# mLSTM cell and tanh-shrink MLP: four more attention units in the split form, another division of the value products, and a re-ranked plan

## The chip, the cores and the metric

One core of a Trainium2 chip. The metric is the device time of one execution in microseconds (us). The kernel before was run three times: 518.15, 518.27 and 518.37 us, median 518.27.

## The reference

Two blocks follow each other. The first is an mLSTM cell over batch 4, 8 heads, 768 steps and head size 40; the second takes the cell's output as 3072 rows of 320 features through two weight matrices with x - tanh(x) between them. All data is float32.

```python
for t in range(S):
    m_new = np.maximum(f_gate[:, :, t] + m, i_gate[:, :, t])
    f_stab = np.exp(f_gate[:, :, t] + m - m_new)
    i_stab = np.exp(i_gate[:, :, t] - m_new)
    C = f_stab * C + i_stab * outer(vt, kt)
    n = f_stab * n + i_stab * kt
    y[:, :, t] = sigmoid(o_gate[:, :, t]) * (C @ qt) / max(abs(n @ qt), 1.0)
x = y.transpose(0, 2, 1, 3).reshape(B * S, H * D)      # (3072, 320)
h = x @ w_in                                           # (3072, 2048)
out = (h - np.tanh(h)) @ w_out                         # (3072, 320)
```

The kernel computes the cell in chunks of 128 steps: scores of queries against keys, masked to earlier steps, times scaled values, plus queries times the state that the earlier chunks left. For small h it takes h - tanh(h) from a polynomial; a branch at the end repeats everything in another way where the bounds do not hold, and is not entered with these inputs.

## The kernel before

**Units.** The cell's work is cut into 24 units: unit n is chunk n // 4 of batch n % 4, all 8 heads, 128 steps. Its steps on TensorE are the scores (`ps`, from `kz` and `qz`), the second products, the update of the state (`pc`, from `k` and the scaled values `vs`), and the turning of the result `ys` into features first, `xT`. DVE or POOL mask the scores into `P`; DVE divides and applies the output gate.

**Two forms.** Units 0 to 11 take the plain form: `inter` and `intra` sum state and values into `ph` (tokens in the rows), `gate` divides, and three transposes on TensorE (`turn`, tile `px`) with a copy (`keep_x`) give `xT`. Units 12 to 23 take the split form: the state is kept with the heads' halves in rows 0 to 39 and 64 to 103; `block_turned` forms values times `P` the other way round (tile `pT`); `turn_back` brings that to tokens in the rows through a round trip by memory (`h_rows`, `z_in`), `gate_turned` divides, and `turn_by_store` makes `xT` by another round trip (`y_rows`). Every one of these transfers is issued on SP's queue. `in_halves` brings the states of the four batches from the plain layout to the split one; it is called four times where the loop begins.

**The MLP.** 12 groups of 256 rows; per group 8 pairs of 128 hidden columns. An item is the up product of one or two pairs (tile `ph_up`): for two pairs 8 products over all 128 rows of the array and 4 over the remaining 64 features, which run in row halves, two at a time. With `quarters`, an item before `block_turned` runs its last part in quarters of the array. The shrink is two squarings on ACT (`z`, `q`) and two products on DVE (`gt`), which also free the banks of `ph_up` for the next item. The down product is `po` (plain) or `pS` (seven products in place of eight, with sums of the weights `wT` and of `gt`, tiles `s`).

**The order.** A helper fixes the order of instructions on each engine to that in which they are written. The first part of it comes from `Plan`: steps with a cost, a rank, their forerunners and the banks that they take are laid out by a small model (`plan.run`, line 1490), and are written out in that order. It covers units 0 to 11, the conversion of the weights (which come as 64-bit numbers) and items 0 to 16. Behind it stands a loop from item 17 (`START`) on, with two items a unit: in the first the new unit is scored after the item's up products, in the second `block_turned` follows the up products. Between the two, line 1510 asks for the loads of the loop's first unit, and lines 1511 and 1512 bring the states into halves:

```python
    load_unit(PLANNED, ("kz", "qz", "v", "k", "o"))
    for b in range(B):
        in_halves(b)
```

Within the loop, the loads of the next unit are asked for at the start of a unit (`cell_slot`).

**Queues.** SP issues the loads of the units and all transfers of the split form, in the written order; an issue whose data is not ready holds what stands behind it. POOL issues the loads of the weights and selects masks for the units in `BY_POOL`. ACT issues most of the output.

**Names in the code.** `weights` and `plan_weights` (conversion, `product` is its last step), `block_turned`, `turn_back`, `turn_by_store`, `in_halves`, `up`, `plan_unit`, `plan_item`, and the constants from line 1182 on.

Of the kernel before, what the change touches and what calls it, by code (L numbers as in the profile page):

```python
# [49 lines left out]
FP = mybir.dt.float32  # L50
# [29 lines left out]
def kernel(  # L80
# [76 lines left out]
    class Plan:  # L157
# [5 lines left out]
        COLD, TURN, WAIT = (6.2, 1.8), 0.12, 0.2188  # L163
# [346 lines left out]
    def weights(dst, srcs, queue):  # L510
# [41 lines left out]
        def product():  # L552
            V.tensor_tensor(out=dst, in0=w["r"], in1=w["e"].bitcast(FP), op=OP.mult)
# [5 lines left out]
    def blocks_of(p):  # L559
# [9 lines left out]
        for i in range(2):  # L569
            whole.append((slice(i * HALF, (i + 1) * HALF), slices(4, 1), moe_w_in[half[i]:half[i] + HALF, slices(2 * p + i, 1)]))  # L570
        return (weights(w_in[:, p, :], whole, G),
                weights(w_out[:, 2 * p:2 * p + 2, :].rearrange("p two n -> p (two n)"),
                        [(every, slice(0, 2 * DM), moe_w_out[slices(2 * p, 2), :].rearrange("(two p) n -> p two n", two=2))], G))
# [40 lines left out]
    def scaled(n, i, name, bufs, by_heads=False):  # L614

        t = un[n]
        flat = att.tile([L, H * D1 + HALF - D1], FP, name=name, tag=name, bufs=bufs)
        to = flat[:, 0:H * D1].rearrange("p (h d) -> p h d", d=D1)
        t["wide"] = flat
        scale = ei[:, i, t["c"], t["hs"]]  # L620
        t["column"] = lambda: A.copy(out=to[:, :, D], in_=scale)
        if by_heads:
            for h in range(H):
                A.mul(out=to[:, h, 0:D], in_=t["v"][:, h], mul=scale[:, h:h + 1])
        else:
            V.tensor_tensor(out=to[:, :, 0:D], in0=t["v"], in1=scale.unsqueeze(2).to_broadcast([L, H, D]), op=OP.mult)
        return to
# [107 lines left out]
    def turn_by_store(n):  # L735
# [6 lines left out]
        V.transpose(flat[:, 0:NK * 128], y[:, 0:NK * 128])  # L742
        V.transpose(flat[:, NK * 128:], y[:, FROM[NK]:])
        rows = dram.tile([(NK + 1) * 128, L], FP, name="y_rows", tag=f"y_rows{n % 4}")
        for a in range(L // BLOCK):
            part = slice(a * BLOCK, (a + 1) * BLOCK)
            SP.dma_start(out=rows[:, part].rearrange("(b i) j -> i b j", i=BLOCK), in_=yt[part])
        for i in range(2):
            half = slice(i * HALF, (i + 1) * HALF)
            SP.dma_start(out=xT[g % NX][half, :, tt * L:(tt + 1) * L], in_=rows.rearrange("(c p) t -> p c t", p=128)[half])  # L750

    def in_halves(b):


        old, new = (state[b][i].rearrange("p h d -> p (h d)") for i in (1, 0))
        for h in (0, 1, 2, 4, 5, 6, 7):
            i, j = divmod(h, HH)
            r = h % TRIO
            n = 2 if h == 0 else 1
            to, at = (x[:, first * D1:(first + TRIO * (n - 1) + 1) * D1].rearrange("p (h d) -> p h d", d=D1)[:, ::TRIO]  # L760
                      for x, first in ((new, j), (old, h)))
            SP.dma_start(out=to[i * HALF:i * HALF + D], in_=at[r * D:(r + 1) * D])

    def block_turned(n):
# [4 lines left out]
        G.memset(t["wide"][:, H * D1:], 0.0)  # L769
        old = state[t["b"]][(t["c"] + 1) % 2].rearrange("p h d -> p (h d)")  # L770

        t["turned"] = [ps_a.tile([128, 2 * 2, L], FP, name="pT", tag=f"a{i}") for i in range(2)]
        for g in range(2):
            for c in range(2):
                for i in range(2):
                    rows, j = slice(i * HALF, i * HALF + D), 2 * g + c
                    T.matmul(t["turned"][i][c * HALF:(c + 1) * HALF, i * 2 + g, :], old[rows, j * D1:j * D1 + HALF], t["qz"][rows, j, :],
                             start=(g == 0), stop=False, skip_group_check=True)
        for i in range(2):
            for g in range(2):  # L780
                for c in range(2):
                    for r in range(2):
                        rows, j = slice(r * HALF, (r + 1) * HALF), 2 * g + c
                        at = (i * HH + j) * D1
                        T.matmul(t["turned"][r][c * HALF:(c + 1) * HALF, i * 2 + g, :], t["wide"][rows, at:at + HALF], t["P"][rows, i, j, :],
                                 start=False, stop=True, skip_group_check=True)
        update_halves(n)

    def update_halves(n):
        t = un[n]  # L790
# [16 lines left out]
    def turn_back(n):  # L807
# [3 lines left out]
        both = att.tile([128, 2, HH * L // BLOCK, BLOCK], FP, name="zt", tag="P", bufs=4)  # L811
        zt, added = both[:, 0], both[:, 1].rearrange("p b i -> p (b i)")
        flat = zt.rearrange("p b i -> p (b i)")
        A.copy(out=added, in_=t["turned"][1].rearrange("p g t -> p (g t)"))
        V.tensor_tensor(out=added, in0=t["turned"][0].rearrange("p g t -> p (g t)"), in1=added, op=OP.add)
        V.transpose(flat, added)
        rows = dram.tile([2, 2, HH, L, BLOCK], FP, name="h_rows", tag=f"h_rows{n % 4}")
        for a in range(128 // BLOCK):
            half, low = divmod(a, 2)
            SP.dma_start(out=rows[low, half].rearrange("g (b k) i -> k (g b) i", k=BLOCK), in_=zt[a * BLOCK:(a + 1) * BLOCK])  # L820
        t["z"] = att.tile([L, 2, H, BLOCK], FP, name="z_in", tag="P", bufs=4)
        for i in range(4):
            part = slice(i * BLOCK, (i + 1) * BLOCK)
            SP.dma_start(out=t["z"][part].rearrange("t a h i -> t (a h) i"),
                         in_=rows.rearrange("a c g t i -> t (a c g) i")[part])
# [27 lines left out]
    def cell_slot(s, o):  # L853
# [16 lines left out]
        steps.append((0.0, lambda: turn_by_store(o)))  # L870
# [152 lines left out]
    def up(some, shrink, quarters=False):  # L1023
# [16 lines left out]
        def quarter(i, x, c):  # L1040
            g, p = some[x]
            rows, cols, first = slice(i * HALF, (i + 1) * HALF), slice(c * HALF, (c + 1) * HALF), 2 * NK * 128 + c * HALF
            T.matmul(ph[i][cols, x, :], w_in[rows, p, first:first + HALF], xT[g % NX][rows, ((0, 2, 1), (0, 1, 2))[i][NK], :],
                     start=False, stop=True, skip_group_check=True)

        full = [(0.43, lambda i=i, x=x, j=j: product(i, x, j)) for i in range(2) for x in range(n) for j in range(NK)]
        if quarters:
            rest = [lambda i=i, x=x, c=c: quarter(i, x, c) for x in range(n) for c in range(2) for i in range(2)]
        else:
            rest = [lambda i=i, x=x: product(i, x, NK) for x in range(n) for i in range(2)]  # L1050
# [132 lines left out]
    SCALED, SHARED = (7, 11), (3, 5, 7, 8, 9, 10, 11)  # L1183
    RANKS = (-1.0, -1.0, -8.2006, -8.4463, 6.0242, 2.3893, 9.5327, 2.6415, 25.6922, 13.6176, 29.7021, 7.061)
    WEIGHTS = (0.08, -0.3563, 5.1266, 7.6972, 9.6586, 11.6503, 11.1391, 25.4848)
    START = item(FIRST * NP)
    HOLD = 43.9795
    FETCH = {(0, 1): 6.75, (2, 1): 12.25, (3, 0): 19.87, (3, 1): 31.49}
    APART = ()
    BY_POOL = (2, 5, 6, 7, 8, 9)  # L1190
# [56 lines left out]
    LATE = {"o": -2.69, "k": -3.541, "q2": -4.0692, "v": -1.3038}  # L1247

    def plan_unit(n, rank):
# [17 lines left out]
        else:  # L1267
# [3 lines left out]
            if c:  # L1271
# [14 lines left out]
        u["scores"] = plan.add("T", 1.0, first_part, [u["qz"], *(of(n - 2, "second") if n in (2, 3) else [])], rank, [(bank, held), ("P", held)], tiles=2, hold=HOLD * (n // B), dense=0.4 if n else 0.6)  # L1286
        if n in BY_POOL:
            copies = [plan.add("A", 0.55, lambda i=i: ready[1][i][0](), [u["scores"]], rank - 6.4275, give=[(bank, held)] if i else ()) for i in range(2)]
            u["mask"] = [plan.add("G", 0.9, lambda i=i: ready[1][i][1](), [copies[i]], rank + 2.098, lag=0.1) for i in range(2)]
        else:  # L1290
            u["mask"] = [plan.add("V", 0.62, lambda i=i: ready[1][i](), [u["scores"]], rank - 1.673, give=[(bank, held)] if i else ())
                         for i in range(2)]
        before = of(n - B, "state")
# [4 lines left out]
        op = None  # L1298

        def second_part(j, heads):  # L1300
            banks[:] = [held["small"]]
            inter(n, j)
            for h in heads:
                intra(n, h)

        parts = TRIOS if c else [range(i * HH, (i + 1) * HH) for i in range(2)]
        for j, heads in enumerate(parts):
            op = plan.add("T", 0.223 * len(heads) + (0.22 if c else 0.0), lambda j=j, heads=heads: second_part(j, heads),
                          ([op] if op else [u["prep"], u["column"], *before, *of(n, "q2") * (c > 0)]) + (u["mask"] if c else u["mask"][j:j + 1]), rank,
                          take=() if op else [("small", held)], give=[("P", held)] if j == len(parts) - 1 else (), dense=0.32)  # L1310
        u["second"] = op
        if shared:
            steps = []
            over = plan.add("V", 0.6, lambda: [steps.extend(gate(n, in_parts=True)), steps[0]()], [op], rank - 0.2851)
            shares = plan.add("A", 1.9, lambda: steps[1](), [over, u["open"]], rank + 9.0221)
            u["gate"] = plan.add("V", 0.5, lambda: steps[2](), [shares, *of(n - 2, "turn")], rank - 7.2476, give=[("small", held)])
        else:
            u["gate"] = plan.add("V", 1.6, lambda: gate(n), [op, u["open"], *of(n - 2, "turn")], rank, give=[("small", held)])

# [7 lines left out]
        def turns():  # L1327
            banks[:] = [held_x["small"]]
            for j in range(NK + 1):
                turn(n, j, at_once=False)  # L1330

        u["turn"] = plan.add("T", 0.35, turns, [u["gate"]], rank, [("small", held_x)], dense=0.5)
# [404 lines left out]
```

## Time and profile before

| | |
|---|---|
| median of three runs | 518.27 us |
| the execution that was profiled | 518.27 us, span 516.6 us |
| DVE busy | 375.5 us (73%) |
| ACT busy | 206.1 us (40%) |
| POOL busy | 37.8 us (7%) |
| granted clock of TensorE | 1.00 over the span |
| up products, `ph_up` | 42% of the chain that ended last |
| seven-product downs, `pS` | 31% |
| plain downs, `po` | 7% |
| second products of the units, `ph` and `pT` | 4% and 3% |
| first product of item 17 | at 203.35 us |

The page gives the busy time of each engine and its share of the span; the chain that ended last is followed back from the last instruction through whatever released each step. In the timeline and the chain, a line is: start in us, length in us, engine, source line (a helper's, so the tiles' names tell what it is), operation, out<-in, shapes, and how many in a row. Each float32 product counts as two instructions, since it runs in two passes.

### The profile page before, as it was taken

What the parts mean: (1) busy time and instruction counts of PE and PEld (TensorE: products, weight loads), DVE (VectorE), ACT (ScalarE), POOL (GpSimd) and SP (SyncE); (2) the same over time, 40 slices, a digit from 0 to 9 for tenths busy, and PEclk for the clock granted to TensorE, in tenths of its full rate; (3) what the DMA queues carried; (4) which work ended last, traced back from release to release, by engine and by line L of the source; (5) the groups of instructions that cost most, each with busy time, mean ns of one, the idle gap of its engine ahead of it and who ended that gap; (6) DMA issues with size and microseconds to landing.
All of it is one profiled execution on the core that took longest, in us unless ns stands there. A gap on an engine that the chain in (4) does not pass through costs nothing.

```text
span 516.6 us, 10519 instructions
## 1 busy us (share of the span) xinstructions
PE 507.4 (98%) x3993; PEld 440.1 (85%) x3993; DVE 375.5 (73%) x828; ACT 206.1 (40%) x523; POOL 37.8 (7%) x75
## 2 busy tenths in 40 slices
PE   8999999999999999999999999999999999999995
PEld 5778878888898888898898899899889899898985
DVE  5999879998856658787768668668668668663734
ACT  4575697666444242242332242232233232232321
POOL 5423234120000000000000000000000000000000
PEclk9999999999999999999999999999999999999999
DMA  7987646340003000033533533533433432310001
GB/s 234 287 253 231 193 141 195 120 113 26 2 4 93 5 27 25 3 81 75 141 70 84 139 73 92 122 81 85 103 81 85 108 81 37 83 30 1 27 0 32
DMA packets 100385, 47.32 MB, mean 92 GB/s; under 512 B 75048, under 2 KB 94056, under 8 KB 100328
## 3 DMA queue, kind: packets, MB, share of 16 engines
q1 hardware_dynamic: 94096, 31.84, 25.7%
q0 software_dynamic: 3040, 10.82, 6.8%
q10 hardware_dynamic: 3192, 3.93, 2.2%
q8 instruction: 33, 0.54, 0.5%
q14 instruction: 24, 0.20, 0.1%
HBM read 36.91 MB, written 9.44 MB: 90 GB/s over the span
## 4 chain that ended last, share of the span: by engine, by line
PE 94%; DMA 2%; ACT 1%; POOL 1%; DVE 0%; issue 0%; SPq 0%; DVEq 0%
PE ph_up L129 42%; PE pS L129 31%; PE po L129 7%; PE ph L129 4%; PE ps L129 4%; PE pT L129 3%; PE pc L129 2%; DMA w<-in_moe_w_in 2%; PE px L133 1%; DMA w_out<-in_i_gate 0%; POOL w L106 0%; ACT vs L106 0%; PE awake L129 0%; ACT L106 0%; DVE w_in L106 0%
## 5 line engine op out<-in xcount | busy, mean ns | idle before, releaser
L129 PE MATMUL ph_up<-xT,w_in 128*128 128x256 f32 (+2 forms) x1248 | 227.5, 387 | 0.0
L129 PEld LDWEIGHTS ph_up<-xT,w_in 128*128 128x128 f32 (+2 forms) x1248 | 173.6, 180 | 36.3 <-issue 15.3
L106 ACT ACTIVATE z<-ph_up 128x512 f32<-128x512 f32 (+1 forms) x98 | 56.8, 583 | 245.9 <-PE ph_up L129 123.7
L106 DVE SCALAR_TENSOR_TENSOR gt<-ph_up,z 128x512 f32<-128x512 f32 (+1 forms) x98 | 63.5, 675 | 67.2 <-ACT z L106 66.9
L129 PE MATMUL pS<-wT,s 128*128 128x160 f32 x480 | 72.0, 299 | 0.0
L129 PEld LDWEIGHTS pS<-wT,s 128*128 128x128 f32 x480 | 67.4, 190 | 0.0
L106 ACT ACTIVATE q<-z,tiny 128x512 f32<-128x512 f32 (+1 forms) x98 | 66.3, 711 | 1.0
L106 DVE SCALAR_TENSOR_TENSOR gt<-q,gt 128x512 f32<-128x512 f32 (+1 forms) x98 | 63.2, 675 | 0.0
L129 PE MATMUL pS<-w_out,gt 128*128 128x160 f32 x320 | 54.3, 312 | 0.0
L106 DVE TENSOR_TENSOR P<-ps,upto 128x512 f32<-128x512 f32 x36 | 23.2, 685 | 41.4 <-PE ps L129 41.4
L129 PEld LDWEIGHTS pS<-w_out,gt 128*128 128x128 f32 x320 | 44.6, 189 | 7.5 <-issue 4.3
L129 PE MATMUL po<-w_out,gt 128*128 128x320 f32 x128 | 38.1, 441 | 0.0
L129 PEld LDWEIGHTS po<-w_out,gt 128*128 128x128 f32 x128 | 23.1, 190 | 8.5 <-issue 0.3
L106 DVE TENSOR_TENSOR s<-gt 128x256 f32<-128x256 f32 x80 | 30.2, 417 | 0.0
L129 PE MATMUL pS<-w_out,s 128*128 128x160 f32 x160 | 28.3, 299 | 0.0
L129 PE MATMUL pS<-wT,gt 128*128 128x160 f32 x160 | 28.3, 299 | 0.0
L129 PEld LDWEIGHTS ps<-qz,kz 40*128 40x128 f32 x384 | 25.1, 188 | 1.7 <-DVE inv L106 0.4
L129 PE MATMUL ps<-qz,kz 40*128 40x128 f32 x384 | 25.9, 274 | 0.0
L129 PEld LDWEIGHTS ph<-vs,P 128*128 128x128 f32 x192 | 23.9, 192 | 1.5 <-POOL P L106 1.1
L129 PE MATMUL ph<-vs,P 128*128 128x41 f32 x192 | 24.4, 273 | 0.6 <-POOL P L106 0.6
L129 PEld LDWEIGHTS pS<-w_out,s 128*128 128x128 f32 x160 | 23.9, 190 | 0.0
L129 PEld LDWEIGHTS pS<-wT,gt 128*128 128x128 f32 x160 | 23.9, 190 | 0.0
(107 smaller groups left out, 488.7 us busy)
## 6 DMA issues: line engine op xcount, KB each, us to landing
w<-in_moe_w_out POOLq DMA_DIRECT2D x8, 640.0 KB, 6.0
w<-in_moe_w_in POOLq DMA_DIRECT2D x16, 256.0 KB, 4.4
kz<-in_kT SPq DMA_DIRECT2D x48, 80.0 KB
o<-in_o_gate SPq DMA_DIRECT2D x24, 160.0 KB
k<-in_k SPq DMA_DIRECT2D x20, 180.0 KB
qz<-in_qT SPq DMA_DIRECT2D x44, 80.0 KB
v<-in_v SPq DMA_DIRECT2D x22, 160.0 KB
out<-ob ACTq DMA_DIRECT2D x11, 320.0 KB
```

The lines of the kernel that those rows point to most:

```text
L106: i = method(*args, **kwargs)
L129: return cls.keep(nc.tensor.matmul(*args, **kwargs))
L133: return cls.keep(nc.tensor.transpose(*args, **kwargs))
```

## The change

1. **Units 8 to 11** take the split form as well, inside the plan (`FLIPPED`). `in_halves` becomes a step of the plan in front of each, with one transfer a head, and the four calls in front of the loop go. Their loads of `q2`, their transposes `px` and their copies go too. A unit is scored only after the loads of `z_in` of the unit before it have been issued. `turn_back` and `turn_by_store` are cut into `blocks`, `stores` and `loads`, each a step of its own.
2. **Values** in all 16 units of the split form: 8 products over all 128 rows and half of the columns, in place of 16 in quarters; the states stay in quarters. The result is in one piece of 2 x 128 columns a bank, so that `turn_back` transposes it straight from the bank (two transposes), without the copy on ACT and the addition on DVE. `quarters` goes from `up`.
3. **The plan**: the third bank of the seven-product runs of groups 0 and 2 is a `small` one, as that of group 3; five products of weights (`ONE_BY_POOL`) go to GpSimd; unit 2 is scored into the up banks; other units are masked by POOL, scaled by heads or gated in shares; every rank is new; `SCORED` gives units 4, 6 and 8 to 11 an earliest time; the plan waits for `xT` of units 8 and 9.
4. The memset of the tail of `vs` goes from POOL (in `block_turned`) to DVE (in `scaled`).

The call `load_unit(PLANNED, ...)` stays where it is, behind `plan.run`.

```diff
-    def weights(dst, srcs, queue):
+    def weights(dst, srcs, queue, by_pool=False):
...
-            V.tensor_tensor(out=dst, in0=w["r"], in1=w["e"].bitcast(FP), op=OP.mult)
+            (G if by_pool else V).tensor_tensor(out=dst, in0=w["r"], in1=w["e"].bitcast(FP), op=OP.mult)
...
+        if n in FLIPPED or n >= PLANNED:
+            V.memset(flat[:, H * D1:], 0.0)
...
     def block_turned(n):
-        G.memset(t["wide"][:, H * D1:], 0.0)
-        t["turned"] = [ps_a.tile([128, 2 * 2, L], FP, name="pT", tag=f"a{i}") for i in range(2)]
+        t["turned"] = [ps_a.tile([128, 2, L], FP, name="pT", tag=f"a{i}") for i in range(2)]
...
-                    T.matmul(t["turned"][i][c * HALF:(c + 1) * HALF, i * 2 + g, :], old[rows, j * D1:j * D1 + HALF], t["qz"][rows, j, :],
+                    T.matmul(t["turned"][i][c * HALF:(c + 1) * HALF, g, :], old[rows, j * D1:j * D1 + HALF], t["qz"][rows, j, :],
                              start=(g == 0), stop=False, skip_group_check=True)
         for i in range(2):
             for g in range(2):
                 for c in range(2):
-                    for r in range(2):
-                        rows, j = slice(r * HALF, (r + 1) * HALF), 2 * g + c
-                        at = (i * HH + j) * D1
-                        T.matmul(t["turned"][r][c * HALF:(c + 1) * HALF, i * 2 + g, :], t["wide"][rows, at:at + HALF], t["P"][rows, i, j, :],
-                                 start=False, stop=True, skip_group_check=True)
+                    j = 2 * g + c
+                    at = (i * HH + j) * D1
+                    T.matmul(t["turned"][i][c * HALF:(c + 1) * HALF, g, :], t["wide"][:, at:at + HALF], t["P"][:, i, j, :],
+                             start=False, stop=True, skip_group_check=True)
...
     def turn_back(n):
-        A.copy(out=added, in_=t["turned"][1].rearrange("p g t -> p (g t)"))
-        V.tensor_tensor(out=added, in0=t["turned"][0].rearrange("p g t -> p (g t)"), in1=added, op=OP.add)
-        V.transpose(flat, added)
...
+        def blocks():
+            for i in range(2):
+                V.transpose(flat[:, i * 2 * L:(i + 1) * 2 * L], t["turned"][i].rearrange("p g t -> p (g t)"))
+        def stores():
+            for a in range(128 // BLOCK):
+                half, low = divmod(a, 2)
+                SP.dma_start(out=rows[low, half].rearrange("g (b k) i -> k (g b) i", k=BLOCK), in_=zt[a * BLOCK:(a + 1) * BLOCK])
+        def loads():
+            t["z"] = att.tile([L, 2, H, BLOCK], FP, name="z_in", tag="P", bufs=4)
+            for i in range(4):
...
-    RANKS = (-1.0, -1.0, -8.2006, -8.4463, 6.0242, 2.3893, 9.5327, 2.6415, 25.6922, 13.6176, 29.7021, 7.061)
+    RANKS = (-1.0, -1.0, -8.7871, -6.9639, 6.9614, 3.5609, 11.868, 3.0007, 1.65, 0.0003, 3.7802, 1.9248)
-    BY_POOL = (2, 5, 6, 7, 8, 9)
+    FLIPPED = (8, 9, 10, 11)
+    FLIPS = (3.0955, -4.5081, 2.7967, 0.1482, -2.8187, -1.6309)
+    SCORED = {4: 26.61, 6: 23.58, 8: 98.4, 9: 133.43, 10: 139.01, 11: 78.31}
+    ONE_BY_POOL = ((0, 1), (2, 1), (3, 0), (5, 1), (6, 1))
+    IN_SMALL = (0, 2, 3)
+    BY_POOL = (2, 5, 6, 9, 11)
...
+        if n in FLIPPED:
+            before = [plan.add("S", 2.8, lambda: in_halves(b), of(n - B, "state"), rank + FLIPS[5])]
...
+            u["second"] = plan.add("T", 1.9, products, [u["prep"], u["column"], *u["mask"], u["k"], *before], rank + FLIPS[0], [("a", banked), ("small", held_c)], [("P", held), ("vs", held)], tiles=3, dense=0.9)
+            blocks = plan.add("V", 0.75, lambda: [backs.extend(turn_back(n)), backs[0]()], [u["second"]], rank + FLIPS[1], [("P", turned)], [("a", banked)])
+            u["update"] = u["state"] = plan.add("V", 0.5, lambda: keep_halves(n), [u["second"], *of_states[c]], rank + FLIPS[2], give=[("small", held_c)])
+            stores = plan.add("S", 2.1, lambda: backs[1](), [blocks], rank - 0.5, give=[("P", turned)])
+            loads = u["loads"] = plan.add("S", 2.1, lambda: backs[2](), [stores], rank - 0.5, [("P", back)])
+            both = plan.add("V", 1.0, lambda: [gates.extend(gate_turned(n)), *[step() for step in gates[:2]]], [loads, u["open"], *of(n - 2, "turn")], rank + FLIPS[3])
+            u["gate"] = plan.add("V", 0.6, lambda: [step() for step in gates[2:]], [both], rank + FLIPS[3], give=[("P", back)])
+            u["turn"] = plan.add("V", 0.65, lambda: [turns_y.extend(turn_by_store(n)), turns_y[0]()], [u["gate"]], rank + FLIPS[4])
+            stores = plan.add("S", 2.1, lambda: turns_y[1](), [u["turn"]], rank - 0.5)
+            u["x"] = plan.add("S", 1.3, lambda: turns_y[2](), [stores], rank - 0.5)
...
+    plan.add("T", 0.0, lambda: None, [units[n]["x"] for n in (FIRST * GT, FIRST * GT + 1)], 1000.0)
...
     load_unit(PLANNED, ("kz", "qz", "v", "k", "o"))
-    for b in range(B):
-        in_halves(b)
...
-            dense, rest = up(some, shrink(x), bool(scored))
+            dense, rest = up(some, shrink(x))
```

## The prediction

> **What bounds the kernel now.** First the page's shares of busy time and the chain that ended last:
> ```profile
> PE 507.4 (98%) x3993; PEld 440.1 (85%) x3993; DVE 375.5 (73%) x828; ACT 206.1 (40%) x523; POOL 37.8 (7%) x75
> PE 94%; DMA 2%; ACT 1%; POOL 1%; DVE 0%; issue 0%; SPq 0%; DVEq 0%
> ```
> TensorE is never without work after the start: 516.6 - 507.4 = 9.2 us are missing, most of them before 6 us and after the last product. So a change is priced by two things: the TensorE work that it adds or removes, and waits that it puts in front of TensorE, whose instructions run in the written order. Next the chain in order of time, for a unit of the plan (start, length, what):
> ```profile
> 98.06 1.71 PE ph L129 x16
> ...
> 100.93 0.60 PE ph L129 x6
> 101.52 0.67 PE pc L129 x6
> ```
> Units 8 to 11 are done like this now, three such rows each, plus half of "55.09 0.66 PE px", which is two units' transposes. Then the timeline of TensorE where the loop begins (item 17; unit 12 scored, then multiplied):
> ```profile
> 207.70 1.06 PE L129 MATMUL ps<-qz,kz 40*128 40x128 f32 x16
> 208.69 1.35 PE L129 MATMUL pS<-w_out,gt 128*128 128x160 f32 x8
> ...
> 217.06 0.62 PE L129 MATMUL pT<-qz,state 40*64 40x128 f32 x16
> 217.50 1.05 PE L129 MATMUL pT<-P,vs 64*64 64x128 f32 x32
> 218.48 0.67 PE L129 MATMUL pc<-vs,k 128*64 128x41 f32 x16
> 219.08 0.40 PE L129 MATMUL pS<-w_out,gt 128*128 128x160 f32 x1
> ```
> From start to start: scores 0.99 us, states 0.44, values 0.98, update 0.60. Last SP's queue, first around the start of the loop, then in a late unit:
> ```profile
> 162.69 0.87 SPq L106 DMA_DIRECT2D kz<-in_kT  x2
> 163.60 0.71 SPq L106 DMA_DIRECT2D qz<-in_qT  x2
> ```
> ```profile
> 299.39 1.89 SPq L106 DMA_DIRECT2D y_rows<-yt  x4
> 302.71 1.24 SPq L106 DMA_DIRECT2D xT<-y_rows  x2
> 304.05 2.18 SPq L106 DMA_DIRECT2D h_rows<-zt  x4
> 307.73 1.90 SPq L106 DMA_DIRECT2D z_in<-h_rows  x4
> 309.67 0.80 SPq L106 DMA_DIRECT2D kz<-in_kT  x2
> 310.51 0.70 SPq L106 DMA_DIRECT2D qz<-in_qT  x2
> 311.26 0.35 SPq L106 DMA_DIRECT2D v<-in_v  x1
> ```
> Unit 12's kz and qz are issued at 162.7 to 164.3, and its scores run at 207.7: 43 us of cover. In a late unit four stores take 2.2 us to issue, and the loads that read them back start 1.5 us after the last (306.23 to 307.73; for y 301.28 to 302.71, 1.4). While SP waits, nothing behind it is issued; the list of waits (total us, times, longest) has it often:
> ```profile
> SPq L106 <- DVE yt L106: 71.5, 12, 8.4
> ```
>
> **Units 8 to 11, on TensorE.** Removed for each: 1.71 + 0.60 + 0.67 + 0.33 = 3.31 us. Added: states 0.44, values, update 0.60, and a change of the array's division on the way in. The values are now 8 products in column halves, two at a time, where 16 quarters ran four at a time: the same streaming, 0.98. A change of division I take from two rows: eight scores two at a time should last half of 16 x 0.107 us (the pace of a 128-column pass, from 1.71/16), 0.86, and take 0.99, so 0.13; an item's 24 up records last 4.51 (302.19 to 306.70) where 8 whole products at 0.433 and 2 steps of 0.427 make 4.32, so 0.19. I use 0.16. So 0.44 + 0.98 + 0.60 + 0.16 = 2.18, and 4 x (3.31 - 2.18) = 4.5 us are saved.
>
> **Units 12 to 23, on TensorE.** The up products' last part is in row halves again and the values in column halves: whole, rows, quarters, columns, whole. Before it was whole, quarters, (columns,) whole. That is one change more for the eight units with an update and two more for the last four, 16 x 0.16 = 2.6 us (2.1 to 3.0). The one new stream that keeps the array awake is 0.2. Net on TensorE: -4.5 + 2.6 + 0.2 = **-1.7 us** (-2.3 to -0.9, with 0.13 and 0.19 for the change of division).
>
> **Work off the path.** One 578 ns copy and one 679 ns addition less per late unit, and the memset on DVE: both engines idle there (DVE 73%, ACT 40% busy), nothing. Five weight products go from DVE (813 to 861 ns) to POOL. No row prices them there; bounds are 1.03 us (its 821 ns select, scaled from 512 to 640 columns) and 1.7 (twice DVE), I take 1.03, as the nearest engine's. The tightest is pair 0's, for the first `po` at 34.29: POOL's fetch ahead of it ended at 29.30, so 31.0 at worst, 3 us of cover. DVE is nearly full there (63.46 of the 70 us from 27 to 97), and items 7 to 11 now come earlier by what the four units leave behind; against that it loses 5 x 0.82 us. I take nothing for this stage, with -0.9 (the one idle gap of TensorE there, 0.86 us before `gate` at 65.98, goes) and +3 (half of the 6.5 us that DVE has left are overdrawn). Ranks, the third bank, shares and masks change order, hardly work. The 32 state transfers cost SP about 0.75 us each (14 in 10.98 us) and are issued before unit 11's loads, with unit 8's products far behind; nothing.
>
> **The seam between plan and loop.** The order of the changed program on SP ends the plan, and begins the loop, so:
> ```
> h_rows<-zt x4 | z_in<-h_rows x4 | y_rows<-yt x4 | xT<-y_rows x2   (unit 11)
> kz<-in_kT x2 | qz<-in_qT x2 | v | k | o                           (unit 12)
> ```
> and on TensorE: unit 11's scores, the 14 products of `pS`, unit 11's states, values and update, then item 17's up products and at once unit 12's scores. `load_unit(PLANNED, ...)` stands behind `plan.run`, so unit 12's kz and qz are queued behind two round trips through memory that wait for unit 11's products. Let 0 be the end of item 16's half products.
> - Unit 12's scores are due at 0.99 (scores 11) + 3.91 (`pS`, 208.69 to 212.60) + 0.16 + 0.44 + 0.98 + 0.60 + 4.52 (item 17) = **11.6**.
> - DVE comes to unit 11's transposes after item 16's shrink and unit 10's gate: 1.0 (up to the first `gt`, 296.26 to 297.27) + two `gt` 1.22 + values 0.57 + ys 0.64 + yt 0.64 + two `gt` 1.22 + four sums 1.7 + the transposes 2 x 0.45 = 7.9. (TensorE alone would allow 7.4.)
> - Then SP 0.1 + 2.18, landing 1.50, loads 1.90, landing; DVE's gate 1.84 (295.33 to 296.92, and 0.25) and yt 0.64; SP 1.89, landing 1.43, xT 1.34, kz and qz 1.54 (309.67 to 311.21), landing. No row shows how long loads take to land; bounds are 1.0 and 2.7 (SP's longest wait for `y_rows`); I take the stores' 1.5, twice. Sum 17.4: qz is there at **25.3**.
>
> So TensorE stands for 25.3 - 11.6 = **13.7 us** (12.2 to 16.1: landings 2 x 1.0 with DVE on time, or 2 x 2.7). Behind the scores in its queue are item 16's `pS` and item 18, so nothing else can fill it. DVE, which waits in the same chain, then has 3.5 us (two masks, four sums, one `gt`) to free item 18's bank, covered by 0.99 + 3.91 of TensorE.
>
> **After the wait.** In this profile the first seven streams are slow, though the granted clock reads 1.00:
> ```profile
> 1.13 2.97 PE L129 MATMUL awake<-diag 128*128 128x512 bf16 x7 [1.13 <-DVE probe L106]
> ...
> 7.51 1.24 PE L129 MATMUL awake<-diag 128*128 128x512 bf16 x5
> ```
> (Two stretches of TensorE's timeline.) That is 0.42 against 0.215 us apiece, some 1.5 us lost. I take 1.5 once more after 13.7 us of idleness; bounds 0 and 1.5. The Trainium skill, "TensorE: Matmul & The Clock Gate", "Part 1: The HAM clock gate", says that the array falls to half clock after about 3.4 us idle and needs about 3.4 us of work to recover; an estimate by it is 1.7 us. No gap of such length is in this trace.
>
> **Sum.** 516.6 - 1.7 + 13.7 + 1.5 = 530.1 us of span. The run profiled took 518.27, which is also the median of the three, so 1.67 lie around the span: **531.8 us**. Own range: 518.27 - 2.3 + 12.2 + 0 - 0.9 = 527.3 to 518.27 - 0.9 + 16.1 + 1.5 + 3 = 538.
>
> **Rivals.**
> - *The seam costs nothing* (faster). If qz were there within 11.6 us of that zero, only -1.7 is left: 516.6 us. For it: the same loads now have 43 us of cover. Against: two round trips would have to shrink by 13.7 us, or SP to pass its waits, which it never does in the trace.
> - *DVE alone holds the seam.* If unit 12's loads were early, DVE would still wait for z_in until 7.9 + 7.2 = 15.1, then gate and yt 2.5, sums 1.3, values 0.6, masks 1.3, sums 1.3, `gt` 0.6: 22.7, where item 18 is due at 11.6 + 4.9 = 16.5: 6.2 us, with 1.5 for the clock 524.3. For it: the same order of instructions; against: the loads are later still.
> - *No change*: the saving eaten by waits of the plan, as DVE is full there, 518.3. It needs the first rival too.
>
> **Chances.** Forecast 0.87, DVE alone 0.05, seam free 0.06, no change 0.02 (0.2%, or 1 us, is about what a measurement of this kernel can tell from none). So faster 0.06, same 0.01, slower 0.93. The range, 526.5 to 537, leaves out both rivals and the forecast's upper end.
>
> **What would show it.** Right: a gap of about 14 us before `ps` near 203 to 217 us, released by a DMA of qz; on SP y_rows, xT, kz, qz in one piece; DVE idle for `z_in` just before; about 199 us for item 17's start (203.35 now, -4.5 + 0.2); late items of a pair longer by 0.16 to 0.3. Wrong: scores of unit 12 without a gap, or gaps before 190 us instead.

## The result, and the profile after

The changed kernel took 542.37 us (median of 6 runs, 537.78 to 546.72) where the kernel before took 518.3 (517.73 to 518.37) beside it: 1.042 times as long, 95% interval 1.036 to 1.049. That ratio is of the means of the runs that count as fast, 540.1 and 518.2 us; the two slowest of the changed kernel, 546.08 and 546.72 us, are left out of it as slow, and the profiled run is the first of these two. The forecast said slower and named the place, but its 531.8 us, and its range up to 537.0, lie too low. The profiled execution has a span of 544.4 us.

The page's shares and the share of the chain that ended last, of the changed kernel:
```profile
PE 520.7 (96%) x3774; PEld 444.8 (82%) x3774; DVE 371.6 (68%) x865; ACT 190.3 (35%) x473; POOL 42.2 (8%) x66
PE 89%; DMA 3%; SPq 3%; DVE 2%; ACT 2%; issue 1%; DVEq 0%; ACTq 0%
```
TensorE is still the bound, but 23.7 us of the span are now without it (9.2 before), and SP's queue has come into the chain with 3% (0% before). Two stretches make up the difference. The first is the seam; TensorE's timeline around it (start, length, what, idle time before and its releaser):
```profile
201.83 1.06 PE L129 MATMUL ps<-qz,kz 40*128 40x128 f32 x16
...
206.82 0.67 PE L129 MATMUL pT<-qz,state 40*64 40x128 f32 x16
207.42 1.09 PE L129 MATMUL pT<-P,vs 128*64 128x128 f32 x16
208.34 0.61 PE L129 MATMUL pc<-vs,k 128*64 128x41 f32 x16
208.89 4.79 PE L129 MATMUL ph_up<-xT,w_in 128*128 128x256 f32 x24
230.23 2.62 PE L129 MATMUL ps<-qz,kz 40*128 40x128 f32 x16 [16.56 <-DMA qz<-in_qT]
232.78 2.50 PE L129 MATMUL pS<-w_out,gt 128*128 128x160 f32 x8
```
Unit 11 is done in 2.07 us here (206.82 to 208.89), near the forecast's 2.18. Then TensorE stands for 16.56 us before unit 12's scores, and the first products behind the gap take twice as long as the same shapes ahead of it (2.62 against 1.06, 2.50 against 1.35). SP's queue over the same stretch has everything in one piece, as forecast:
```profile
205.45 1.85 SPq L106 DMA_DIRECT2D y_rows<-yt  x4
210.48 1.24 SPq L106 DMA_DIRECT2D xT<-y_rows  x2
211.84 2.14 SPq L106 DMA_DIRECT2D h_rows<-zt  x4
215.57 1.90 SPq L106 DMA_DIRECT2D z_in<-h_rows  x4
221.67 1.86 SPq L106 DMA_DIRECT2D y_rows<-yt  x4
225.03 1.24 SPq L106 DMA_DIRECT2D xT<-y_rows  x2
226.31 0.90 SPq L106 DMA_DIRECT2D kz<-in_kT  x2
227.25 0.71 SPq L106 DMA_DIRECT2D qz<-in_qT  x2
```
The first two rows are unit 10's, the next four unit 11's, the last two unit 12's. DVE's row at this place ends "9.05 <-DMA z_in<-h_rows": it waits in the same chain.

The second stretch is the start. TensorE issues the same instructions there in the same order as before, but:
```profile
8.95 2.34 PE L129 MATMUL awake<-diag 128*128 128x512 bf16 x5
...
28.27 2.29 PE L129 MATMUL awake<-diag 128*128 128x512 bf16 x5
30.40 1.88 PE L129 MATMUL ph<-vs,P 128*128 128x41 f32 x16
```
Five streams took 1.24 us at 7.51 in the kernel before; here they take 2.3 until 28 us. From one stream to the next it is 427 ns at first in both kernels and 216 ns later, from 3.9 us on before, and only from about 30 us on here. So item 0 starts at 32.78 us, where it was 22.37.

The start is a matter of the single run. The same kernel measured again (12 runs in all) lies at 534.5 to 539.4 us eight times and at 545 to 546.7 four times. In the last column below is a profile of it with a good start. Each row is taken from the starts of items in TensorE's timeline, less the same stretch of the kernel before (there item 17 starts at 203.19 us; the 203.35 given further up is the chain's figure):

| stretch | forecast, us | profiled run | profiled again |
|---|---|---|---|
| up to item 0 | 0 | +10.4 | -0.5 |
| item 0 to item 17 (units 8 to 11, the plan) | -4.3 | -4.7 | -4.8 |
| item 17 to 18: the gap | +13.7 | +16.6 | +16.1 |
| item 17 to 18: the rest, mostly slow products | +1.5 | +3.0 | +3.3 |
| item 18 to 48 (late units) | +2.6 | +3.0 | +3.0 |
| behind item 48 | 0 | -0.4 | -0.9 |
| span | +13.5 | +27.8 | +16.2 |

### The profile page after: what moved, and what is told of

It is laid out like the page before. It is cut to its first block, busy times and chain, and to the rows that moved or that the text cites. A ratio compares the mean times of both kernels' runs of the same rounds, so it can differ in the third digit from the quotient of the medians.

```text
span 544.4 us, 10118 instructions
## 1 busy us (share of the span) xinstructions
PE 520.7 (96%) x3774; PEld 444.8 (82%) x3774; DVE 371.6 (68%) x865; ACT 190.3 (35%) x473; POOL 42.2 (8%) x66
## 3 DMA queue, kind: packets, MB, share of 16 engines
q1 hardware_dynamic: 117696, 34.85, 27.8%
## 4 chain that ended last, share of the span: by engine, by line
PE 89%; DMA 3%; SPq 3%; DVE 2%; ACT 2%; issue 1%; DVEq 0%; ACTq 0%
PE ph_up L129 38%; PE pS L129 29%; PE po L129 6%; PE ps L129 5%; PE pT L129 4%; PE awake L129 3%; PE ph L129 3%; SPq L106 3%; PE pc L129 1%; DMA y_rows<-yt 1%; PE px L133 1%; DMA qz<-in_qT 1%; DMA k<-in_k 0%; DMA z_in<-h_rows 0%; ACT z L106 0%
## 5 line engine op out<-in xcount | busy, mean ns | idle before, releaser
L129 PE MATMUL ph_up<-xT,w_in 128*128 128x256 f32 (+1 forms) x1152 | 227.3, 388 | 0.0
L129 PEld LDWEIGHTS ph_up<-xT,w_in 128*128 128x128 f32 (+1 forms) x1152 | 175.8, 189 | 35.5 <-issue 15.1
L106 DVE TENSOR_TENSOR P<-ps,upto 128x512 f32<-128x512 f32 x38 | 24.6, 684 | 54.1 <-PE ps L129 54.1
L129 PE MATMUL pS<-w_out,gt 128*128 128x160 f32 x320 | 55.5, 317 | 0.0
L129 PE MATMUL ps<-qz,kz 40*128 40x128 f32 x384 | 30.1, 300 | 16.6 <-DMA qz<-in_qT 16.6
L129 PEld LDWEIGHTS ps<-qz,kz 40*128 40x128 f32 x384 | 28.7, 210 | 19.2 <-issue 17.3
L106 POOL DMA_DIRECT2D w<-in_moe_w_in x32 | 18.5, 585 | 30.5 <-DVE w_e L106 26.8
L106 ACT ACTIVATE o<-o 128x320 f32<-128x320 f32 x24 | 11.3, 470 | 26.4 <-DMA o<-in_o_gate 26.3
```

The lines of the kernel that those rows point to most:

```text
L106: i = method(*args, **kwargs)
L129: return cls.keep(nc.tensor.matmul(*args, **kwargs))
```

## Experiments

**Unit 12's loads early.** They go ahead of unit 10's y stores, where SP waits for DVE:
```
-            stores = plan.add("S", 2.1, lambda: turns_y[1](), ...)
+            ahead = n == PLANNED - 2
+            stores = plan.add("S", 2.1, lambda: [ahead and load_unit(PLANNED, ("kz", "qz", "v", "k", "o")), turns_y[1]()], ...)
...
-    load_unit(PLANNED, ("kz", "qz", "v", "k", "o"))
```


> Unit 12's five loads are issued ahead of unit 10's y stores, in a stretch where SP waits for DVE; nothing else moves. Theory (the seam is two waits, one behind the other: SP's queue first, DVE's wait for unit 11's z_in second): the 16.6 us gap before ps goes, and a gap of about 7.5 us opens before item 18's ph_up, because DVE still stands for z_in and reaches item 17's cubes only 2.5 (gate and yt) + 1.1 (four sums) + 0.6 + 1.3 (values, masks) + 1.1 + 0.65 us later; with 1.5 to 3 us of slow clock after it that is 527.3 to 528.8 us where the changed kernel has 537.8. Rival (SP's queue alone held the seam): no gap is left, 518.3 us. Rival (the loads were not what ps waited for): the gap stays, 537.8 us.

Measured: 527.53 us (525.25 to 537.52). TensorE's timeline, and under it DVE's, of this kernel:
```profile
204.65 1.06 PE L129 MATMUL ps<-qz,kz 40*128 40x128 f32 x16
...
209.00 0.71 PE L129 MATMUL pS<-w_out,s 128*128 128x160 f32 x4
217.41 7.52 PE L129 MATMUL ph_up<-xT,w_in 128*128 128x256 f32 x24 [7.70 <-DVE gt L106]
```
```profile
210.47 0.17 DVE L106 SCALAR_TENSOR_TENSOR den<-z_in,inv 128x8 f32<-128x8 f32 x1 [9.20 <-DMA z_in<-h_rows]
...
216.58 1.28 DVE L106 SCALAR_TENSOR_TENSOR gt<-ph_up,z 128x512 f32<-128x512 f32 x2
```
The scores have no wait now, and the second wait comes out as expected (about 7.5): 7.70 us before item 18, whose bank DVE frees with the `gt` at 216.58, behind its 9.20 us for z_in. So the seam was two waits, one hidden by the other. The up products behind the gap take 7.52 us where they take 4.68: the slow pace costs 2.84 here, without any load that TensorE waits for.

**Unit 11's tail in the loop as well.** Its gate, transposes, y stores and xT loads leave the plan; the loop's first slot does them:
```
+            if n == PLANNED - 1:
+                return
             both = plan.add("V", 1.0, lambda: [gates.extend(gate_turned(n)), ...
...
-    slots = [tuple(n if PLANNED <= n < NU else None for n in (s, s - 1)) ...
+    slots = [tuple(n if PLANNED - 1 <= n < NU else None for n in (s, s - 1)) ...
```


> Besides unit 12's early loads, unit 11's gate, transposes, y stores and xT loads leave the plan and are spread over the loop's first slot, as every later unit's are over its own. Theory: the seam is then free: item 18 starts 9.4 us after item 17, as in the loop, and 19.5 us are gone: 537.8 - 19.5 = 518.3 us, which is the kernel before minus 4.6 (units 8 to 11) plus 3.0 (late units), plus some 1.6 us that the fast start of the changed kernel still has too much. Rival (the seam only moves: something of unit 11 is late for the loop): a gap of more than 2 us somewhere between 208 and 240 us, over 520 us. A second claim, of the two groups of times (537.8 to 539.4 and 545.4 to 546.7 us): if they come from the start, where the profiled run has TensorE at half pace until 30 us, this kernel has two groups some 7.5 us apart too; if they come from the long gap, it has one group.

Measured: item 18 starts 9.52 us after item 17 (28.96 in the changed kernel), and the list of TensorE's waits has nothing there; all of it is:
```profile
PE awake L129 <- DVE probe L106: 1.1, 1, 1.1
PE pc L129 <- DMA k<-in_k: 0.7, 1, 0.7
PE px L133 <- DVE ys L106: 0.2, 1, 0.2
```
Two runs took 516.17 and 516.38 us, two 525.21 and 526.15. The seam is worth 19.4 us (28.96 - 9.52). That two groups some 9 us apart remain, without any long gap, says that the gap does not make them.

**The late units' quarters back.** On top of that, units 12 to 23 as in the kernel before:
```
+                    for r in range(2 * late):
+                        rows = slice(r * HALF, (r + 1) * HALF)
+                        T.matmul(t["turned"][r][c * HALF:(c + 1) * HALF, i * 2 + g, :], t["wide"][rows, at:at + HALF], t["P"][rows, i, j, :], ...)
...
-            dense, rest = up(some, shrink(x))
+            dense, rest = up(some, shrink(x), bool(scored))
```


> As the run before it, and units 12 to 23 get back their value products in quarters of the array and the quarters in the up products' last part, as in the kernel before; units 8 to 11 keep column halves. Theory (each change of the array's division costs about 0.16 to 0.19 us, 2.97 us measured over the late items): 2.97 us less than the run before it, 515.3 us, and pairs of late items back at 9.41 + 10.39 us, below the kernel before's 518.3. Rival (the late items got longer for another cause, such as waits for the banks): their pairs stay at 9.41 + 10.59 us, no difference.

Measured: 513.67 to 524.57 us, median 516.53, with all pairs of items back at 9.41 + 10.39 (9.41 + 9.79 for the last four units). From item 18 to 48 it takes 285.43 us, as in the kernel before; the changed kernel takes 288.39. Measured again in more runs:

> The version with unit 12's early loads, unit 11's tail in the loop and late quarters once more, with more rounds. Theory: units 8 to 11 save 4.6 us and nothing else is left of the change, so its shortest time is 4.6 us (4.0 to 5.0) below the shortest of the kernel before, 513.7 against 518.1. Rival (the saving is given back at the seam or by waits of the plan): shortest time within 1 us of the kernel before's.

512.99 us (512.88 to 513.35, 6 runs), 0.9875 of the kernel before beside it (0.9836 to 0.9914), whose 12 runs spread from 517.59 to 529.41. Between the shortest times lie 4.7 us, where the forecast gave units 8 to 11 4.5 (4.3 with the added stream). The version keeps the new order of the plan as well, so its time alone does not say which of the two saves. TensorE's own time between items 0 and 17, by tile, does: from the kernel before to this version `ph`, `px` and `pc` lose 11.2 us and `pT` gains 6.1, which is -5.1 for the units; all the rest together adds about 0.3. All six runs lie below the shortest of the kernel before, so this version beats both kernels, by a little over 1%.

**Streams in the gap.** 74 streams between item 17's last up product and unit 12's scores:
```
+                for step in rest[0]:
+                    step()
+                stream(ps_a.tile([128, 512], FP, name="awake", tag="a0"), 74)
+                part = scores(n[0])
```


> The changed kernel with 74 streams that keep the array busy (74 x 0.2156 = 15.95 us) between item 17's last up product and unit 12's scores, in a bank that is free there. Theory (after the gap TensorE runs at half pace for a while, 2.99 us lost, because it had been idle): the scores take 1.06 us again where they took 2.62, the pS products 1.35 where they took 2.50, and item 18 starts 25.9 to 26.1 us after item 17 where it was 28.96: 534.8 us against 537.8. Rival (the products are slow there because of the loads that run beside them): scores still about 2.6 us, 537.8 us.

Measured (TensorE's timeline of this kernel):
```profile
204.94 16.15 PE L129 MATMUL awake<-diag 128*128 128x512 bf16 x74
223.04 0.46 PE L129 MATMUL ps<-qz,kz 40*128 40x128 f32 x2 [1.96 <-DMA qz<-in_qT]
224.18 1.13 PE L129 MATMUL ps<-qz,kz 40*128 40x128 f32 x14 [0.68 <-issue]
225.24 1.35 PE L129 MATMUL pS<-w_out,gt 128*128 128x160 f32 x8
```
The pace holds, as the theory has it: 1.35 us for the first eight `pS`, not 2.50, with loads beside them that keep the DMA engines as busy as there (busy for 0.83 of the time around these products, 0.74 in the changed kernel). The time does not gain: 537.13 us (533.23 to 537.99), item 18 at 28.92. The data came later this time, as SP waited 3.2 us for unit 11's y_rows (it was 1.5 in the changed kernel's profile), and the scores stopped once more, for 0.68 us, for a reason that the profile does not show. So idleness as the cause of the slow products is shown, a shorter time by streams is not.

**Only the tail in the loop,** with unit 12's loads where the change has them:

> The changed kernel with unit 11's gate, transposes, y stores and xT loads moved into the loop, and unit 12's loads left where they are, behind unit 11's z_in loads on SP. Theory (both round trips of unit 11 stood in front of kz and qz): only the first is left, so kz and qz are issued some 5.6 us after item 17's up products end on SP, qz is there 7 to 8 us after the scores are due, the gap before ps is 7 to 8 us (16.56 with both), half pace after it costs 2.8 to 3.0 us as after the 7.70 us gap, and item 18 starts 19.3 to 20.5 us after item 17 (28.96 in the changed kernel, 9.52 with a free seam); no second gap behind it, about 526 to 527 us with a start like the kernel before's. Rival (the wait for z_in on DVE is the one that matters, so that taking it away frees the seam): no gap over 2 us, 516.2 us.

Measured:
```profile
210.36 2.50 PE L129 MATMUL ps<-qz,kz 40*128 40x128 f32 x16 [7.02 <-DMA qz<-in_qT]
```
7.02 us of gap, item 18 19.92 us after item 17, 528.55 us (526.19 to 538.07). One round trip in front of kz and qz is worth 7.0 us of gap, both 16.1 to 16.6. With this the two halves of the seam are told apart: either edit alone leaves 7 to 8 us of gap, both together none.

**The start.** The changed kernel unaltered, beside the kernel before:

> The changed kernel, unaltered, beside the others. Theory (its time is 535.5 us with a start like that of the kernel before's trace, and what is above that is the start's half pace): times from 533 to 546 us, and the kernel before, which has the same first instructions on TensorE, spreads in the same way above 518 us; in the trace item 18 starts 28 to 30 us after item 17, whatever the start. Rival (what makes it 537 to 547 us belongs to the change): the kernel before stays within 1 us of 518.3 while this one spreads over 9 us.

536.14 us (534.51 to 544.96), ratio 1.033 (1.028 to 1.038); its trace is the table's last column. The kernel before spread from 517.59 to 529.41 beside it, so the spread is not the change's own. Then the burst of streams at the start, first in the best version:
```
-        stream(spare[0], n)
+        begun_bursts.append(n)
+        stream(spare[0], {1: 18, 2: 0}.get(len(begun_bursts), n))
```


> The version with unit 12's early loads, unit 11's tail in the loop and late quarters, and its first burst of streams made 18 long where it was 10; the second burst (5 streams) is left out. Theory (the start runs at half pace for 3 to 28 us, by chance, and goes to full pace only after some 3.4 us of unbroken streams that happen to fall well): cold streams come 427 ns apart and full ones 216, so 18 streams hold the array for at least 6 us, every run is at full pace by 8 or 9 us, item 0 starts between 22 and 25 us in all of them, and the times lie within 3 us of each other, about 513.7 to 516.7 us. Rival (the half pace at the start does not depend on the streams): times still spread over 8 to 11 us, with some at 523 or above.

514.59 us (514.09 to 515.6, 7 runs). All within 1.5 us, but the same version with the short burst was within 0.5 beside it, so this tells nothing by itself. Hence the same edit in both kernels, and the opposite one, no early streams, in the kernel before:

> The kernel before with its first burst of streams made 18 long where it was 10, the second (5) left out. Theory (the runs of one kernel spread over 9 us because TensorE stays at half pace for up to 28 us at the start, which an unbroken burst of more than twice 3.4 us cannot miss): all times within 3 us, 518.5 to 521.5 us, while the unaltered kernel beside it keeps times above 522. Rival (the spread comes from something else, so the burst does not touch it): some of its times are above 525 us, as often as the unaltered kernel's.

> The kernel before without its first two bursts (no streams until 9 us). Theory: no stretch of 3.4 us is unbroken work at the start, so nearly every run stays at half pace (streams 427 ns apart) past 15 us, item 0 starts between 26 and 33 us, and the times lie at 522 to 529 us. Rival (the first bursts do not decide the pace): times like the unaltered kernel's, most of them at 518 us.

> The changed kernel with the same long first burst. Theory: item 18 still starts 28 to 30 us after item 17 (the seam), and the times keep within 3 us of each other, 535.5 to 538.5 us, none near 545. Rival (the long gap makes the spread): times still spread over 8 us, some at 543 or above.

The kernel before, unaltered, gave 518.02 to 528.80 in 22 runs. With the long burst it gave 519.21 to 520.27 eight times and 524.4 to 526.17 four times: a miss for the theory as it was put, though times above 525 us are as rare with it (one of 12) as without (two of 22). Without bursts it gave 526 us or more in 9 of 11 runs (median 526.5). So the bursts do bear on the pace, but a long one does not hold it. The trace of the long burst shows why (first rows of TensorE's timeline):
```profile
1.12 5.46 PE L129 MATMUL awake<-diag 128*128 128x512 bf16 x18 [1.12 <-DVE probe L106]
...
8.88 1.75 PE L129 MATMUL ps<-qz,kz 40*128 40x128 f32 x16 [0.27 <-DVE P L106]
10.56 2.10 PE L129 MATMUL awake<-diag 128*128 128x512 bf16 x5
```
18 streams in 5.46 us: the pace went to full in the burst (granted clock 1.00 from 3.99 us). Then, after 4 us of gates and scores with small waits, the next five streams take 2.10 us: it has dropped again (granted clock 0.50 from 10.81 to 24.47 us). The changed kernel with the long burst took 536.4 to 542.52, with its seam at 29.14 us; three of its six runs are above the expected 538.5, and the spread of 6.1 us lies between the theory's 3 and the rival's 8.

What decides in a given run whether the pace is held stays open. The traces give one sign: in every profile here, each recorded stretch of granted clock that ends within the run lasts a whole number of times 3.41 us (6.83 and 13.65 in this trace, 17.07 in the changed kernel's gap), so the clock changes only at steps that far apart, and the first change falls elsewhere in each profile (3.77 us in the kernel before, 3.99 in this trace, 5.99 and 30.39 in the two of the changed kernel). If a step must be busy enough as a whole, it matters by chance where the steps fall; no run sets that, so it is not shown. Nor is it known why the kernel before had none of this in its first six runs; it spread in each of the three later measurements, which were on three different chips.

## Why the prediction was right, and where it failed

**What failed, in short.** Two terms of the sum were sized too low, the seam (13.7 us, measured 16.56) and the slow products after it (1.5, measured 3.0); with these and the other terms as measured, the sum is 535.8 us, still inside the range. The third step carried the time out of the range: the start was put at nothing, and cost 10.4 us in the profiled run.

**The mechanism of the seam was right**: SP's order puts unit 12's kz and qz behind two round trips, TensorE stands once, before `ps`, released by qz, and DVE waits in the same chain. The rival of the free seam falls with the 16.56 us; that of DVE alone falls too, but what it described is real: with the loads early it appeared, 7.70 us where the rival's working gave 6.2.

**Step "the seam", sized too low: 13.7 us, measured 16.56 (16.10 again).** With the same zero (201.83, the start of unit 11's scores) the forecast's terms and the trace's stand so: scores due 11.6, found 11.8 (213.67); transposes done 7.9, found 7.7 (209.55). But "then SP 0.1" took SP to be free. It was not: unit 10's xT loads still stood in front of unit 11's stores and waited until 210.48 for y_rows, 3.2 us after the last store where 1.4 to 1.5 is common, so the stores began at 211.84, 2.2 us late. The forecast had no term for this, because the queue was followed from unit 11 on only. The last landing, of qz, took 2.27 us (227.96 to 230.23) where 1.5 was taken: 0.8. These two are 3.0 of the 3.1 us by which qz came later than forecast (28.4 after the zero, not 25.3; the other terms add up to 0.1). The scores were themselves due 0.2 later, which leaves the 2.9 that the gap has too much.

**Step "after the wait", 1.5 us, sized too low: measured 3.0, 3.3 and 3.6 behind gaps of 16 us, 3.5 behind one of 7.0 and 2.84 behind one of 7.7.** (About 0.1 of each but the last is the other division of item 17's products: a free seam takes 9.52 us, not 9.41.) The upper bound came from the start, where the pace happened to recover after seven streams. The granted clock in stretches of 2 us (the figure before the DMA share; columns: stretch and its length, busy PE, PEld, DVE, ACT, POOL) shows how long it lasts:
```profile
216.00:218.00 2.00, 0.00 (x0) 0.00 (x0) 0.00 (x0) 0.00 (x0) 0.00 (x0) 1.00 0.55 90
218.00:220.00 2.00, 0.00 (x0) 0.00 (x0) 0.66 (x4) 0.00 (x0) 0.00 (x0) 0.53 0.26 41
...
232.00:234.00 2.00, 2.00 (x11) 1.78 (x9) 1.50 (x3) 1.34 (x4) 0.00 (x0) 0.50 0.92 294
234.00:236.00 2.00, 2.00 (x12) 2.00 (x12) 1.97 (x7) 1.51 (x4) 0.00 (x0) 0.70 0.25 91
236.00:238.00 2.00, 2.00 (x16) 2.00 (x16) 1.97 (x6) 0.29 (x1) 0.00 (x0) 1.00 0.00 0
```
It falls to 0.50 at about 218 us, more than 4 us into the gap, and comes back at about 235, some 5 us after work was resumed. In the five profiles with a gap of 7 us or more, the clock fell 2.3 to 4.7 us after the last product and came back 5.0 to 6.7 us after the first, and somewhat over half of that last time is lost. The Trainium skill, "TensorE: Matmul & The Clock Gate", "Part 1: The HAM clock gate", has at least one window of about 3.4 us for both. The way back was longer than one window each time, so the estimate worked out from it, 1.7, was too low as the row's 1.5 was; the fall came sooner than one window in three of the five (2.3, 2.9 and 3.1 us), and there the measurement decides.

**Step "units 12 to 23", 2.6 us, measured 2.96**: 0.19 to 0.20 for each of eight units and 0.35 for each of the last four, so 0.185 a change of division on average, near the upper of the two rows that the forecast had (0.13 and 0.19), not their mean. A late unit of the changed kernel:
```profile
297.84 4.68 PE L129 MATMUL ph_up<-xT,w_in 128*128 128x256 f32 x24
302.45 0.67 PE L129 MATMUL pT<-qz,state 40*64 40x128 f32 x16
303.05 1.09 PE L129 MATMUL pT<-P,vs 128*64 128x128 f32 x16
303.97 0.61 PE L129 MATMUL pc<-vs,k 128*64 128x41 f32 x16
304.52 1.35 PE L129 MATMUL pS<-w_out,gt 128*128 128x160 f32 x8
```
From start to start: up products 4.61 us, states 0.60, values 0.92, update 0.55, where item 18 and unit 12 of the kernel before take 4.46, 0.44, 0.98 and 0.60. That the difference belongs to the two edits in these units is shown by the run with the late quarters back. That it is a price per change of division is worked out from the sums alone; no run isolates one change.

**Step "units 8 to 11", -4.5 us: nearly right.** Items 0 to 17 got 4.7 to 4.8 us shorter (4.3 forecast with the added stream), and the version that keeps these units and the plan is 4.7 us below the kernel before. Unit 11 takes 2.07 us, not 2.18; for four units that is 0.4, the rest of the difference.

**Work off the path: hidden, as said, though one price was wrong.** The weight products on POOL last 1.66 us (mean of four) and 1.91 (one), not 1.03, and the one is above the bound of 1.7 too; the cover that the forecast named was enough, and TensorE's one wait before the seam is 0.65 us for a `k` load. No stall of the plan beyond that.

**The start was not in the forecast at all.** This is the term, put at nothing, that takes the measured time out of the range. Its first sign stood in the profile before (seven slow streams), read as a constant of the kernel; that "the granted clock reads 1.00" there was no sign against it, as that trace has no record of the clock before 3.77 us. Up to item 0 the two profiles of the changed kernel differ by 10.9 us (+10.4 and -0.5). Without it the forecast's sum with the measured terms, 518.27 - 4.7 + 16.6 + 3.0 + 3.0 - 0.4, is 535.8 us, near which eight of the twelve runs of the changed kernel lie (534.5 to 539.4). That early streams bear on the start is shown; why it goes well in one run and not in the next stays open.

## What to carry to other kernels

When a step joins an in-order queue, follow that queue from the step ahead of it, with the longest landing that the trace shows: a wait that has slack today becomes the start time of everything behind it. A stall can hide a second one on another engine, and then either cure alone gets back only part (8.7 and 9.0 of 19.4 us here: 28.96 - 17.38 - 2.84, and 28.96 - 19.92); price the rival for the case that the first wait is gone, too. And where a planned part hands over to a loop, give the last planned unit's tail and the first looped unit's loads to the form that the loop uses for all others.

## What was not expected of the hardware

- TensorE can stay at half pace (427 ns from stream to stream, 216 otherwise) for 29 us of work without a gap, as from 1.13 to about 30 us in the changed kernel's profile. The column of the granted clock reads 1.00 there, but only because the trace has no record of the clock before 30.39 us, just where the pace becomes full; where there is a record, as in the long burst's trace from 3.99 us on, the column shows the 0.50. So the pace at the start is read from equal instructions, not from that column.
- From SP's last store to the first load that reads it back, 1.4 to 1.6 us pass in most places. For y_rows it is 2.4 to 3.5 us in three to five of 16 cases in each kernel with units 8 to 11 in the split form, and in none or one of 12 in each profile of the kernel before, with or without bursts. No cause was found.
